# The end of two dense layers on one core: other order of the matmul passes, the last unit in two blocks, another engine for the last store

## The chip, the core and the metric

The kernel runs on one core of a Trainium2 chip. TensorE (PE) does the matrix products, and loads its weights beside them (PEld); VectorE (DVE), ScalarE (ACT) and GpSimd (POOL) do the elementwise work, SyncE (SP) issues most DMAs. Each engine takes its own instructions in the order in which they are written. The metric is the device time of one execution in microseconds (us); the kernel before takes 1350.9 us, the median of 3 runs (1350.5 to 1351.06).

## What is computed

A long convolution by Fourier transforms gives 12480 rows of 128 columns. Two dense layers follow, each of 128 to 2048 to 128:

```python
def _moe_ref(x, w_in, w_out):
    h = np.maximum(x @ w_in, 0.0)
    return (h * h @ w_out).astype(np.float32)

def _moe2_ref(x, w_in, w_out):
    h = x @ w_in
    alpha = 1.0
    g = np.where(h > 0.0, h, alpha * (np.exp(np.minimum(h, 0.0)) - 1.0))
    return (g @ w_out).astype(np.float32)
```

## The kernel before

The change lies in `phase3`, which does both dense layers. The 12480 rows are cut into NT = 25 tiles of 512 columns of the transposed data; the last tile has 334. The 2048 hidden values of a tile are done in 8 units of 256, two blocks of 128 partitions in one PSUM tile `[128, 2, n]`. So each layer has NS = 200 units.

An operand in float32 is split into a part in fp32r, hi, and the rest, lo. One product of a unit is six matmuls (`mm6`, L190 to L195): for each of the two blocks high weights by hi and low weights by hi, which makes four, and then high weights by lo for each block, which makes the last two, passes 4 and 5 (counted from 0). The first product of a unit writes `h` (`mm1`), the second adds to `y` over 8 units (`mm2`); `y` is the output of the tile. For the last tile of layer 2 the second product is not split: two matmuls in plain float32 with the whole weights `wl` (L783).

The elementwise work of one unit of layer 2, with its lines: ACT makes `tn` = tanh(h/2) (L827) and `ex` = exp(h) (L828); DVE makes `em` = (ex + 1) * tn in the place of tn (L887), which is exp(h) - 1, and `g` = max(min(em, 0), h) in the place of ex (L913); ACT copies g to fp32r, `hi` (L170); `lo` = g - hi is made by DVE, or one block by POOL and one by DVE at the end (L167). Layer 1 has r, g, hi and lo of its own (L895, L899, L906, L167).

One loop runs over s. Iteration s does unit s of layer 1 and unit k = s - 11 of layer 2, so that from s = 200 on (`both` is false) only layer 2 is left, in the units 189 to 199. In one iteration the units of layer 2 stand at four stages: the first product of k (`mid(k)`), em and g of k - 1 (`pa`), hi and lo of k - 2 (`pb`), and the second product of k - 3 (`pc`). The last tile of layer 2 is the units 192 to 199.

The order in which the code is written is the order on each engine (the schedule is manual). Two things in it matter here. `mid(k)` stands at the end of an iteration, or, where `end` is true (k from 194 on), right behind the second product of k - 3 and ahead of the elementwise work. And `lo_of` takes an argument `after`: an artificial wait of the subtraction until `em` of this iteration is done.

The PSUM tiles for h in layer 2 come from a pool of two (`h2`) and, for every third unit of the last 8 (`third`), from a third tile (`h`) that layer 1 no longer needs. The last column tile is copied out of PSUM by ACT (`fin`, L170) and stored by a DMA that SP issues (L803).

Of the kernel before, what the change touches and what calls it, by code (L numbers as in the profile page):

```python
# [14 lines left out]
AF = mybir.ActivationFunctionType  # L15
ALU = mybir.AluOpType
# [19 lines left out]
NT = len(SIZES) - 1  # L36
# [13 lines left out]
LO0 = 8  # L50
# [106 lines left out]
class Build:  # L157
# [29 lines left out]
    def big(self, i, dt=F32):  # L187
        return self.wp.tile([128, (4096, 4096, 8192)[i]], dt, tag=f"m{i}", name=f"m{i}")

    def mm6(self, outs, w, hi, lo, first, last):  # L190
        one = outs[0] is outs[1]
        seq = [(b, h, x) for b in range(2) for h, x in ((0, hi), (1, hi))] + [(b, 0, lo) for b in range(2)]
        for i, (b, h, x) in enumerate(seq):
            self.nc.tensor.matmul(outs[b], lhsT=w[:, b, h], rhs=x[b], start=first and i in ((0,) if one else (0, 2)),  # L194
                                  stop=last and i in ((5,) if one else (4, 5)))  # L195

# [467 lines left out]
    def phase3(self):  # L664
        nc, a = self.nc, self.a
        ctx0 = self.ctx
        with ExitStack() as self.ctx:
            gh = self.pool("gh3", 3)
            gp = self.pool("gp3", 2)
# [76 lines left out]
                    xin[t, 0] = (xh, xl)  # L746
                yield

            def mm1(t, l, u, odd=False):
                n, ne = width(t)  # L750
                xh, xl = xin[t, l]
                w = self.w[l, 0]
                if odd:
                    hs = spare()
                elif l == 0:
                    hs = psh.tile([128, 2, 512], F32, tag="h", name="h")
                else:
                    hs = pair.pop("s")
                self.mm6([hs[:, b, :ne] for b in range(2)], w[:, 2 * u:2 * u + 2], [xh[:, :ne]] * 2, [xl[:, :ne]] * 2,
                         True, True)  # L760
                return hs[:, :, :ne]

            def pairs(pool, nm, t, dt=F32):
                return pool.tile([128, 2, 512], dt, tag=nm, name=nm)[:, :, :width(t)[1]]
# [6 lines left out]
                        self.tc.add_manual_dep(i.ins, after.ins.name, SYNC, reason="lo beside the reads of h")  # L771
                st["lo"] = lo

            def mm2(t, l, u, hi, lo):
                n, ne = width(t)
                w = self.w[l, 1]
                if u == 0:
                    nm = f"y{l if t < NT - 1 else 0}"
                    yps[t, l] = psy.tile([128, 512], F32, tag=nm, name=nm)
                y = yps[t, l][:, :ne]  # L780
                if lo is None:
                    for b in range(2):
                        nc.tensor.matmul(y, lhsT=wl[:, 2 * u + b], rhs=hi[:, b, :ne], start=(u + b == 0),  # L783
                                         stop=(u + b == 8))
                    return
                self.mm6([y, y], w[:, 2 * u:2 * u + 2], [hi[:, b, :ne] for b in range(2)],
                         [lo[:, b, :ne] for b in range(2)], u == 0, u == 7)

            def fin(t, l):
                n, ne = width(t)  # L790
                y = yps[t, l]
                if l == 0:
                    xh, xl = row(xp, "xh1", F32R), row(xp, "xl1", F32R)
                    self.copy(xh[:, :ne], y[:, :ne])
                    yield
                    self.sub(nc.vector, xl[:, :ne], y[:, :ne], xh[:, :ne].bitcast(F32))
                    xin[t, 1] = (xh, xl)
                    return
                if t < NT - 3:
                    yield  # L800
                ys = row(ld, "ys")
                self.copy(ys[:, :n], y[:, :n])
                nc.sync.dma_start(out=self.outs(t), in_=ys[:, :n])  # L803

            seq = [(t, u) for t in range(NT) for u in range(8)]
            NS = len(seq)
# [14 lines left out]
            def mid(k, own):  # L821
                if not 0 <= k < NS:
                    return
                pair["s"] = own
                t2, u2 = seq[k]
                e = two[k] = {"t": t2, "h": mm1(t2, 1, u2), "tn": pairs(gp, "tn", t2), "ex": pairs(gh, "ex", t2)}
                nc.scalar.activation(out=e["tn"], in_=e["h"], func=AF.Tanh, scale=0.5)  # L827
                nc.scalar.activation(out=e["ex"], in_=e["h"], func=AF.Exp)  # L828

            def whole(q):  # L830
                w = self.w[1, 1][:, 2 * q:2 * q + 2].bitcast(F32)
# [6 lines left out]
            one, two = {}, {}  # L838
# [4 lines left out]
            for s in range(NS + LEAD + 2):  # L843
                k = s - LEAD
                m = s - LAG1
                both = s < NS
                pa, pb, pc = (two.get(k - i) for i in (1, 2, 3))
                pair.pop("s", None)
                pair["late"] = not both
                end = NS - 6 <= k < NS  # L850
                own = None
                if 0 <= k < NS:
                    third = k >= NS - 8 and k % 3 == (NS - 7) % 3
                    own = psh.tile([128, 2, 512], F32, tag="h", name="h") if third else spare()
                if both:
                    t, u = seq[s]
                    if own is not None:
                        pair["s"] = own
                    if (t, u) in loads:
                        load(loads[t, u])  # L860
                    if (t, u) in preps:
                        bg.append(prep(preps[t, u]))
                step()
                if both:
                    f = one[s] = {"t": t, "h": mm1(t, 0, u, k < 0 and (s == 1 or s > 0 and s % 2 == 0))}
                while post:
                    post.pop(0)()
                if 0 <= m < NS:
                    e = one.pop(m)
                    mm2(e["t"], 0, seq[m][1], e["hi"], e["lo"])  # L870
                if pc:
                    two.pop(k - 3)
                    mm2(pc["t"], 1, seq[k - 3][1], pc["hi"], pc["lo"])
                    if seq[k - 3][1] == 7:
                        late.append((pc["t"], 1))
                if end:
                    mid(k, own)
                if pb and pb["t"] == NT - 1:
                    two.pop(k - 2)
                    mm2(pb["t"], 1, seq[k - 2][1], pb["g"], None)  # L880
                    if seq[k - 2][1] == 7:
                        late.append((pb["t"], 1))
                    pb = None
                after = None
                if pa:
                    pa["em"] = pa["tn"]
                    after = nc.vector.scalar_tensor_tensor(out=pa["em"], in0=pa["ex"], scalar=1.0, in1=pa["tn"],  # L887
                                                           op0=ALU.add, op1=ALU.mult)
                if s - 1 in one:
                    lo_of(one[s - 1], "lo0", nc.gpsimd if s > LO0 else nc.vector, after=after)  # L890
                if both and t == 3:
                    whole(u)
                if both:
                    f["r"] = pairs(gp, "r", t)
                    nc.scalar.activation(out=f["r"], in_=f["h"], func=AF.Relu)  # L895
                step()
                if both:
                    f["g"] = pairs(gp, "g", t)
                    nc.vector.scalar_tensor_tensor(out=f["g"], in0=f["h"], scalar=0.0, in1=f["r"],  # L899
                                                   op0=ALU.max, op1=ALU.mult)  # L900
                if pb:
                    pb["hi"] = pairs(gh, "hi1", pb["t"], F32R)
                    self.copy(pb["hi"], pb["g"])
                if both:
                    f["hi"] = pairs(gh, "hi0", t, F32R)
                    nc.scalar.activation(out=f["hi"], in_=f["r"], func=AF.Square)  # L906
                if 0 <= m < NS and m % 8 == 7:
                    finish(seq[m][0], 0)
                if not both and pb:
                    lo_of(pb, "lo1", nc.gpsimd, (0,), after)  # L910
                if pa:
                    pa["g"] = pa["ex"]
                    nc.vector.scalar_tensor_tensor(out=pa["g"], in0=pa["em"], scalar=0.0, in1=pa["h"],  # L913
                                                   op0=ALU.min, op1=ALU.max)
                while low:
                    next(low.pop(0), 0)
                if pb:
                    lo_of(pb, "lo1", nc.vector, (slice(0, 2) if both else 1,))
                for x in late:
                    finish(*x)  # L920
                late = []
                if not end:
                    mid(k, own)
# [44 lines left out]
```

## Time and profile before

| | |
|---|---|
| median of 3 runs | 1350.9 us |
| the profiled execution | 1351.62 us |
| its span in the trace | 1349.8 us |
| PE busy | 1337.2 us, 99% of the span |
| DVE busy | 1173.7 us, 87% |
| ACT busy | 1118.8 us, 83% |
| POOL busy | 621.6 us, 46% |

The profiled execution lasted 1351.62 us; its trace spans 1349.8 us, so 1.8 us lie outside the trace. Times in rows are us from the start of the span. A matmul's end is modelled; of the matmuls therefore their starts are read. A number in brackets at the end of a row is the time for which the engine stood idle before the instruction, and whose end released it.

### The profile page before, as it was taken

The page shows a single profiled execution, that of the slowest core. Times are in us where ns is not written, and L with a number is a line of the kernel's source. Part 1 is how long each engine was busy: PE and PEld are TensorE (multiplying, and loading weights), DVE is VectorE, ACT ScalarE, POOL GpSimd, SP SyncE. Part 2 cuts the span into 40 slices and gives each one's busy share as a digit, 9 for nine tenths or more (in the row PEclk, how much of TensorE's full clock was granted, in tenths as well). Part 3 has the DMA queues.
Part 4 walks back from the last instruction along what each step waited for, and adds up shares of the span by engine and source line. Part 5 has one row for each costly group of instructions (what it writes and reads, how often), then busy time and mean ns, then how long its engine had stood idle before and what let it go on. Part 6 is the DMA issues. An engine that isn't in the chain of part 4 may idle for free.

```text
span 1349.8 us, 18810 instructions
## 1 busy us (share of the span) xinstructions
PE 1337.2 (99%) x6958; PEld 1113.9 (83%) x6958; DVE 1173.7 (87%) x1190; ACT 1118.8 (83%) x1435; POOL 621.6 (46%) x364
## 2 busy tenths in 40 slices
PE   9999999999999999999999999999999999999998
PEld 9987777898888888888888888888888888888885
DVE  6659996889989898998899889988998989898997
ACT  6678775788888898889888888988898888888885
POOL 3027780455744444444444444444444445444531
PEclk9999999999999999999999999999999999999999
DMA  8747775401110111011011101110111011100000
GB/s 253 222 138 218 217 232 155 130 3 51 52 46 7 52 52 37 17 53 53 22 31 52 53 9 44 53 52 1 53 53 49 4 53 53 35 2 9 8 8 14
DMA packets 71338, 89.36 MB, mean 66 GB/s; under 512 B 5579, under 2 KB 62790, under 8 KB 71246
## 3 DMA queue, kind: packets, MB, share of 16 engines
q1 hardware_dynamic: 71102, 88.03, 21.9%
q8 instruction: 55, 0.90, 0.3%
q14 instruction: 37, 0.30, 0.1%
q10 hardware_dynamic: 144, 0.13, 0.0%
HBM read 69.78 MB, written 18.32 MB: 65 GB/s over the span
## 4 chain that ended last, share of the span: by engine, by line
PE 91%; DMA 5%; DVE 2%; SPq 1%; issue 0%; ACT 0%; POOL 0%; DVEq 0%; ACTq 0%; POOLq 0%
PE h L194 38%; PE y L194 38%; PE v L527 3%; PE u L504 3%; PE s L318 3%; DMA m<-in_xv_dram 2%; PE h L376 2%; PE h L645 2%; PE h L649 2%; PE rt L363 1%; DMA z<-Zd 1%; DMA xr<-in_post_dram 1%; PE y L783 1%; DVE tn L887 0%; DVE lo L167 0%
## 5 line engine op out<-in xcount | busy, mean ns | idle before, releaser
L167 POOL TENSOR_TENSOR lo<-g,hi 128x1024 fp32r<-128x1024 f32 (+2 forms) x192 | 467.8, 2437 | 599.9 <-DVE tn L887 495.9
L194 PE MATMUL h<-xh,m 128*128 128x512 f32 (+3 forms) x1600 | 421.3, 385 | 3.4 <-DVE g L899 2.3
L194 PE MATMUL y<-hi,m 128*128 128x512 f32 (+2 forms) x1568 | 419.0, 389 | 0.0
L194 PEld LDWEIGHTS h<-xh,m 128*128 128x128 f32 x1600 | 298.6, 188 | 62.4 <-DVE g L899 3.3
L194 PEld LDWEIGHTS y<-hi,m 128*128 128x128 f32 x1568 | 290.0, 188 | 59.2 <-ACT ys L170 4.7
L827 ACT ACTIVATE tn<-h 128x1024 f32<-128x1024 f32 (+3 forms) x200 | 201.5, 1008 | 151.5 <-PE h L194 151.5
L887 DVE SCALAR_TENSOR_TENSOR tn<-ex,tn 128x1024 f32<-128x1024 f32 (+3 forms) x200 | 240.3, 1201 | 99.7 <-ACT ex L828 98.3
L167 DVE TENSOR_TENSOR lo<-ex,hi 128x1024 fp32r<-128x1024 f32 (+3 forms) x192 | 248.1, 1292 | 0.0
L899 DVE SCALAR_TENSOR_TENSOR g<-h,r 128x1024 f32<-128x1024 f32 (+3 forms) x200 | 238.2, 1191 | 9.3 <-ACT r L895 9.3
L194 PE MATMUL y<-lo,m 128*128 128x512 f32 (+2 forms) x784 | 240.4, 387 | 2.1 <-POOL lo L167 1.6
L194 PE MATMUL h<-xl,m 128*128 128x512 f32 (+3 forms) x800 | 242.1, 384 | 0.0
L913 DVE SCALAR_TENSOR_TENSOR ex<-tn,h 128x1024 f32<-128x1024 f32 (+3 forms) x200 | 236.7, 1184 | 1.8 <-DVE tn L887 0.5
L906 ACT ACTIVATE hi<-r 128x1024 fp32r<-128x1024 f32 (+3 forms) x200 | 209.8, 1049 | 0.5
L895 ACT ACTIVATE r<-h 128x1024 f32<-128x1024 f32 (+3 forms) x200 | 202.4, 1012 | 8.3 <-PE h L194 6.9
L170 ACT ACTIVATE hi<-ex 128x1024 fp32r<-128x1024 f32 (+2 forms) x192 | 203.8, 1062 | 0.0
L828 ACT ACTIVATE ex<-h 128x1024 f32<-128x1024 f32 (+3 forms) x200 | 199.6, 998 | 0.0
L194 PEld LDWEIGHTS y<-lo,m 128*128 128x128 f32 x784 | 146.6, 188 | 34.6 <-POOL lo L167 3.7
L194 PEld LDWEIGHTS h<-xl,m 128*128 128x128 f32 x800 | 149.5, 188 | 28.5
L519 POOL TENSOR_TENSOR pt<-pt 127x256 f32<-127x256 f32 x43 | 33.5, 779 | 88.4 <-DVE pt L516 88.3
L516 DVE TENSOR_TENSOR pt<-u,hh 127x512 f32<-127x512 f32 (+1 forms) x46 | 31.2, 679 | 21.4 <-PE u L504 20.5
L527 PE MATMUL v<-pt,g 127*128 127x512 f32 (+1 forms) x92 | 48.5, 612 | 0.0
L724 DVE SCALAR_TENSOR_TENSOR v<-z,sg 118x384 f32<-118x384 f32 (+3 forms) x75 | 43.0, 573 | 0.0
(87 smaller groups left out, 1058.9 us busy)
## 6 DMA issues: line engine op xcount, KB each, us to landing
Zd<-z SPq DMA_DIRECT2D x45, 256.0 KB
z<-Zd SPq DMA_DIRECT2D x48, 192.0 KB
z<-Zd SPq DMA_DIRECT2D x48, 136.5 KB
xc<-in_xv_dram SPq DMA_DIRECT2D x16, 392.0 KB
tb<-in_tf_dram SPq DMA_DIRECT2D x46, 127.0 KB
out_dram<-ys SPq DMA_DIRECT2D x22, 256.0 KB
raw<-in_moe_w_in_dram SPq DMA_DIRECT2D x8, 512.0 KB
raw<-in_moe_w_out_dram SPq DMA_DIRECT2D x8, 512.0 KB
```

The costliest lines, as they stand in the source:

```text
L167: return eng.tensor_tensor(out=out, in0=a, in1=b, op=ALU.subtract)
L170: self.nc.scalar.activation(out=out, in_=in_, func=AF.Copy)
L194: self.nc.tensor.matmul(outs[b], lhsT=w[:, b, h], rhs=x[b], start=first and i in ((0,) if one else (0, 2)), stop=last and i in ((5,) if on ...
L527: nc.tensor.matmul(v, lhsT=self.g[:N2], rhs=pt.rearrange("p j r d -> p (j r d)"), start=True, stop=True)
L724: nc.vector.scalar_tensor_tensor(out=v[:k, i, q], in0=zi[:, :, 1], scalar=self.sg[:k, i:i + 1], in1=zi[:, :, 0], op0=ALU.mult, op1=ALU.add)
L827: nc.scalar.activation(out=e["tn"], in_=e["h"], func=AF.Tanh, scale=0.5)
L828: nc.scalar.activation(out=e["ex"], in_=e["h"], func=AF.Exp)
L887: after = nc.vector.scalar_tensor_tensor(out=pa["em"], in0=pa["ex"], scalar=1.0, in1=pa["tn"], op0=ALU.add, op1=ALU.mult)
L895: nc.scalar.activation(out=f["r"], in_=f["h"], func=AF.Relu)
L899: nc.vector.scalar_tensor_tensor(out=f["g"], in0=f["h"], scalar=0.0, in1=f["r"], op0=ALU.max, op1=ALU.mult)
L906: nc.scalar.activation(out=f["hi"], in_=f["r"], func=AF.Square)
L913: nc.vector.scalar_tensor_tensor(out=pa["g"], in0=pa["em"], scalar=0.0, in1=pa["h"], op0=ALU.min, op1=ALU.max)
```

## The change

The order of instructions differs from the iteration s = 200 on; ahead of it nothing moves.

- Once layer 1 is done (`both` false), the second product of k - 3 is cut in two: its four hi passes, then `mid(k)`, then its two lo passes.
- `end` is true from k = 190 on, not from 194, so that `mid(k)` stands ahead of the elementwise work in four more iterations. The third PSUM tile is used from k = 190 on.
- `after` is left out for lo of layer 1's last unit.
- The last unit (199) is done block by block: its first product in the order of passes 0, 1, 4, 2, 3, 5, then tn and ex of block 0 and of block 1, then em and g of block 0 and of block 1.
- The last store is issued by ACT, not by SP.

```diff
-    def mm6(self, outs, w, hi, lo, first, last):
+    def mm6(self, outs, w, hi, lo, first, last, passes=range(6)):
         one = outs[0] is outs[1]
         seq = [(b, h, x) for b in range(2) for h, x in ((0, hi), (1, hi))] + [(b, 0, lo) for b in range(2)]
-        for i, (b, h, x) in enumerate(seq):
+        for i in passes:
+            b, h, x = seq[i]
...
-                nc.sync.dma_start(out=self.outs(t), in_=ys[:, :n])
+                (nc.sync if t < NT - 1 else nc.scalar).dma_start(out=self.outs(t), in_=ys[:, :n])
...
-                e = two[k] = {"t": t2, "h": mm1(t2, 1, u2), "tn": pairs(gp, "tn", t2), "ex": pairs(gh, "ex", t2)}
-                nc.scalar.activation(out=e["tn"], in_=e["h"], func=AF.Tanh, scale=0.5)
-                nc.scalar.activation(out=e["ex"], in_=e["h"], func=AF.Exp)
+                order = (0, 1, 4, 2, 3, 5) if k == NS - 1 else range(6)
+                e = two[k] = {"t": t2, "h": mm1(t2, 1, u2, passes=order), "tn": pairs(gp, "tn", t2),
+                              "ex": pairs(gh, "ex", t2)}
+                for b in blocks(k):
+                    nc.scalar.activation(out=e["tn"][:, b], in_=e["h"][:, b], func=AF.Tanh, scale=0.5)
+                    nc.scalar.activation(out=e["ex"][:, b], in_=e["h"][:, b], func=AF.Exp)
+
+            def blocks(k):
+                return (0, 1) if k == NS - 1 else (slice(0, 2),)
+
+            def minmax(e, b):
+                nc.vector.scalar_tensor_tensor(out=e["g"][:, b], in0=e["em"][:, b], scalar=0.0, in1=e["h"][:, b],
+                                               op0=ALU.min, op1=ALU.max)
...
-                end = NS - 6 <= k < NS
+                end = NS - 10 <= k < NS
                 own = None
                 if 0 <= k < NS:
-                    third = k >= NS - 8 and k % 3 == (NS - 7) % 3
+                    third = k >= NS - 10 and k % 3 == (NS - 7) % 3
...
                 if pc:
                     two.pop(k - 3)
-                    mm2(pc["t"], 1, seq[k - 3][1], pc["hi"], pc["lo"])
+                    mm2(pc["t"], 1, seq[k - 3][1], pc["hi"], pc["lo"], range(6) if both else range(4))
+                if end:
+                    mid(k, own)
+                if pc:
+                    if not both:
+                        mm2(pc["t"], 1, seq[k - 3][1], pc["hi"], pc["lo"], (4, 5))
                     if seq[k - 3][1] == 7:
                         late.append((pc["t"], 1))
-                if end:
-                    mid(k, own)
...
-                    after = nc.vector.scalar_tensor_tensor(out=pa["em"], in0=pa["ex"], scalar=1.0, in1=pa["tn"],
-                                                           op0=ALU.add, op1=ALU.mult)
+                    pa["g"] = pa["ex"]
+                    for b in blocks(k - 1):
+                        after = nc.vector.scalar_tensor_tensor(out=pa["em"][:, b], in0=pa["ex"][:, b], scalar=1.0,
+                                                               in1=pa["tn"][:, b], op0=ALU.add, op1=ALU.mult)
+                        if k == NS:
+                            minmax(pa, b)
                 if s - 1 in one:
-                    lo_of(one[s - 1], "lo0", nc.gpsimd if s > LO0 else nc.vector, after=after)
+                    lo_of(one[s - 1], "lo0", nc.gpsimd if s > LO0 else nc.vector, after=after if both else None)
```

On TensorE, in the iterations k = 190 and 191, there stood before (y1 is the output of tile 23, hi1 and lo1 are the parts of one unit, and h2_12016 and h2_12050 the first products of units 190 and 191):

```order
L194 MATMUL y1_11909<-hi1_12000,m2_2011 128x512 x4
L194 MATMUL y1_11909<-lo1_12002,m2_2011 128x512 x2
L194 MATMUL h2_12016<-xh1_11698,m2_2011 128x512 x4
L194 MATMUL h2_12016<-xl1_11699,m2_2011 128x512 x2
L194 MATMUL y1_11909<-hi1_12030,m2_2011 128x512 x4
L194 MATMUL y1_11909<-lo1_12035,m2_2011 128x512 x2
L194 MATMUL h2_12050<-xh1_11698,m2_2011 128x512 x4
```

and there stands now (h_12016 and h2_12050 are the same two products; hi1_12040 is what hi1_12030 was):

```order
L195 MATMUL y1_11909<-hi1_12000,m2_2011 128x512 x4
L195 MATMUL h_12016<-xh1_11698,m2_2011 128x512 x4
L195 MATMUL h_12016<-xl1_11699,m2_2011 128x512 x2
L195 MATMUL y1_11909<-lo1_12002,m2_2011 128x512 x2
L195 MATMUL y1_11909<-hi1_12040,m2_2011 128x512 x4
L195 MATMUL h2_12050<-xh1_11698,m2_2011 128x512 x4
L195 MATMUL h2_12050<-xl1_11699,m2_2011 128x512 x2
```

The lo passes have moved from ahead of h to behind it. Between the six matmuls of h_12016 and the hi passes that need hi1_12040 two matmuls are left; the hi passes stand directly ahead of the next h.

On ScalarE, in the same iterations, there stood before:

```order
L827 ACTIVATE tn_12012<-h2_11984 128x1024
L828 ACTIVATE ex_12013<-h2_11984 128x1024
L170 ACTIVATE hi1_12030<-ex_11981 128x1024
L170 ACTIVATE xh1_12032<-y0_11723 128x334
L827 ACTIVATE tn_12046<-h2_12016 128x1024
L828 ACTIVATE ex_12047<-h2_12016 128x1024
L170 ACTIVATE hi1_12058<-ex_12013 128x1024
```

and there stands now:

```order
L831 ACTIVATE tn_12012<-h2_11984 128x1024
L832 ACTIVATE ex_12013<-h2_11984 128x1024
L831 ACTIVATE tn_12033<-h_12016 128x1024
L832 ACTIVATE ex_12034<-h_12016 128x1024
L170 ACTIVATE hi1_12040<-ex_11981 128x1024
L170 ACTIVATE xh1_12042<-y0_11723 128x334
L831 ACTIVATE tn_12061<-h2_12050 128x1024
```

The copy hi1 of unit 188 (from ex_11981, which holds its g) stood ahead of tn and ex of unit 190; now it stands behind them. The same holds in the three iterations that follow (hi1_12068, hi1_12092, hi1_12116).

On VectorE, at the very end, two rows over both blocks stood before:

```order
L887 SCALAR_TENSOR_TENSOR tn_12199<-ex_12200,tn_12199 128x2x334
L913 SCALAR_TENSOR_TENSOR ex_12200<-tn_12199,h2_12192 128x2x334
L887 SCALAR_TENSOR_TENSOR tn_12214<-ex_12215,tn_12214 128x2x334
L913 SCALAR_TENSOR_TENSOR ex_12215<-tn_12214,h_12207 128x2x334
L962 UNCONDITIONAL_BRANCH
```

and now four stand there:

```order
L838 SCALAR_TENSOR_TENSOR ex_12200<-tn_12199,h2_12192 128x2x334
L903 SCALAR_TENSOR_TENSOR tn_12214<-ex_12215,tn_12214 128x334
L838 SCALAR_TENSOR_TENSOR ex_12215<-tn_12214,h_12207 128x334
L903 SCALAR_TENSOR_TENSOR tn_12214<-ex_12215,tn_12214 128x334
L838 SCALAR_TENSOR_TENSOR ex_12215<-tn_12214,h_12207 128x334
```

The last unit's em and g are made for block 0 and then for block 1.

## Rows read from the trace of the kernel before

**Rows 1.** Part 1 of the page: busy us, share of the span, instructions.

```profile
PE 1337.2 (99%) x6958; PEld 1113.9 (83%) x6958; DVE 1173.7 (87%) x1190; ACT 1118.8 (83%) x1435; POOL 621.6 (46%) x364
```

**Rows 2.** Busy time by stretch: us; PE, PEld, DVE, ACT, POOL; PEclk granted clock; DMA, GB/s.

```profile
1320.00:1324.00 4.00, 3.26 (x13) 2.10 (x12) 3.11 (x4) 3.70 (x5) 1.29 (x1) 1.00 0.00 0
...
1347.00:1349.80 2.80, 0.00 (x0) 0.00 (x0) 0.00 (x0) 0.07 (x1) 0.00 (x0) 1.00 0.17 61
```

**Rows 3.** Timeline, PE and ACT, units 190 and 191: start, us, instruction, idle before.

```profile
1317.42 1.09 PE L194 MATMUL h<-xh,m 128*128 128x512 f32 x4
...
1318.81 1.08 PE L194 MATMUL y<-hi,m 128*128 128x512 f32 x4
1319.01 1.03 ACT L827 ACTIVATE tn<-h 128x1024 f32<-128x1024 f32 x1 [1.79 <-PE h L194]
...
1319.94 1.01 ACT L828 ACTIVATE ex<-h 128x1024 f32<-128x1024 f32 x1
...
1320.62 1.09 PE L194 MATMUL h<-xh,m 128*128 128x512 f32 x4
1320.83 1.06 ACT L170 ACTIVATE hi<-ex 128x1024 fp32r<-128x1024 f32 x1
...
1322.00 1.15 PE L194 MATMUL y<-hi,m 128*128 128x512 f32 x4
```

**Rows 4.** Timeline, PE and ACT, units 192 to 194, 334 columns.

```profile
1325.73 0.73 ACT L827 ACTIVATE tn<-h 128x668 f32<-128x668 f32 x1 [0.64 <-PE h L194]
1326.36 0.72 ACT L828 ACTIVATE ex<-h 128x668 f32<-128x668 f32 x1
...
1326.96 1.06 ACT L170 ACTIVATE hi<-ex 128x1024 fp32r<-128x1024 f32 x1
...
1327.80 0.77 PE L194 MATMUL h<-xh,m 128*128 128x334 f32 x4
...
1328.71 1.08 PE L194 MATMUL y<-hi,m 128*128 128x512 f32 x4
...
1330.58 0.77 PE L194 MATMUL h<-xh,m 128*128 128x334 f32 x4
```

**Rows 5.** Timeline, POOL, DVE and PE, end of layer 1.

```profile
1308.89 1.64 POOL L167 TENSOR_TENSOR lo<-g,hi 128x668 fp32r<-128x668 f32 x1 [2.94 <-DVE tn L887]
...
1310.56 1.22 DVE L167 TENSOR_TENSOR lo<-ex,hi 128x1024 fp32r<-128x1024 f32 x1
...
1311.96 0.63 PE L194 MATMUL y<-lo,m 128*128 128x512 f32 x2
...
1312.10 1.23 DVE L887 SCALAR_TENSOR_TENSOR tn<-ex,tn 128x1024 f32<-128x1024 f32 x1 [0.33 <-ACT ex L828]
...
1313.79 0.77 PE L194 MATMUL y<-hi,m 128*128 128x334 f32 x4
...
1315.06 1.75 POOL L167 TENSOR_TENSOR lo<-ex,hi 128x512 fp32r<-128x512 f32 x1
...
1315.16 0.57 PE L194 MATMUL y<-lo,m 128*128 128x334 f32 x2 [0.60 <-POOL lo L167]
...
1315.97 1.92 DVE L887 SCALAR_TENSOR_TENSOR tn<-ex,tn 128x1024 f32<-128x1024 f32 x1 [0.32 <-ACT ex L828]
```

**Rows 6.** Timeline: the only DMA that ACT issues, and the last instructions.

```profile
0.73 0.40 ACTq L266 DMA_DIRECT2D xt<-in_wz_dram  x1
...
1342.24 0.85 DVE L913 SCALAR_TENSOR_TENSOR ex<-tn,h 128x668 f32<-128x668 f32 x1
...
1343.33 0.85 DVE L887 SCALAR_TENSOR_TENSOR tn<-ex,tn 128x668 f32<-128x668 f32 x1 [0.24 <-ACT ex L828]
1344.29 0.85 DVE L913 SCALAR_TENSOR_TENSOR ex<-tn,h 128x668 f32<-128x668 f32 x1
...
1345.20 1.39 PE L783 MATMUL y<-ex,wl 128*128 128x334 f32 x4 [0.66 <-DVE ex L913]
...
1347.10 0.33 SPq L803 DMA_DIRECT2D out_dram<-ys  x1
```

More of the change, by code (lines that the diff above doesn't have):

```diff
@@ L747, in prep, with mm1 @@
                 yield
-            def mm1(t, l, u, odd=False):
+            def mm1(t, l, u, odd=False, passes=range(6)):
                 n, ne = width(t)
@@ L759, in mm1 @@
                 self.mm6([hs[:, b, :ne] for b in range(2)], w[:, 2 * u:2 * u + 2], [xh[:, :ne]] * 2, [xl[:, :ne]] * 2,
-                         True, True)
+                         True, True, passes)
                 return hs[:, :, :ne]
@@ L772, in lo_of, with mm2 @@
                 st["lo"] = lo
-            def mm2(t, l, u, hi, lo):
+            def mm2(t, l, u, hi, lo, passes=range(6)):
                 n, ne = width(t)
                 w = self.w[l, 1]
-                if u == 0:
+                if u == 0 and 0 in passes:
                     nm = f"y{l if t < NT - 1 else 0}"
@@ L786, in mm2 @@
                 self.mm6([y, y], w[:, 2 * u:2 * u + 2], [hi[:, b, :ne] for b in range(2)],
-                         [lo[:, b, :ne] for b in range(2)], u == 0, u == 7)
+                         [lo[:, b, :ne] for b in range(2)], u == 0, u == 7, passes)
             def fin(t, l):
@@ L910, in phase3 @@
                     lo_of(pb, "lo1", nc.gpsimd, (0,), after)
[L911 to L914, printed above, removed]
+                if pa and k < NS:
+                    minmax(pa, slice(0, 2))
                 while low:
```

## The prediction

> **What bounds the kernel now.** I read the page's busy shares first: PE is busy 99% of the span, and the next engine, DVE, 87% [rows 1]. For most of the span the time is PE's own work, and there the change moves nothing. So I went to the last 40 us, by stretches. In the four us from 1320 PE is busy for 3.26, with 13 matmuls, beside 3.70 of ACT [rows 2]: here PE waits for the elementwise engines, and an order matters. Then I read the timeline of this stretch, to see for each wait what ended last.
>
> Two places carry the argument. At the end of layer 1 PE reaches the lo passes of layer 1 and waits for POOL: the hi passes start at 1313.79, the lo passes only at 1315.16, released by POOL's lo [rows 5]. And in the units behind, each iteration of layer 2 is a loop through three engines, whose lengths stand in the timeline: the first product starts at 1317.42, its tn on ACT at 1319.01, ex at 1319.94, a hi copy at 1320.83, and the hi passes that read this copy start at 1322.00 [rows 3]. That is 4.58 us from the h of unit 190 to the hi passes that read the copy behind its tn and ex. Today PE fills this with the hi and lo passes of another unit and with the h of unit 191, which starts at 1320.62 [rows 3]. The reader is to see that PE loses little here because a whole h stands between the two.
>
> **The change part by part.**
>
> *The four iterations k = 190 to 193.* Because `mid` is ahead of the elementwise work there, ACT now does tn and ex of unit k first and the hi copy of unit k - 2 behind them. PE, in the next iteration, needs that very copy for its first four matmuls, and the h of unit k + 1 stands behind these. So a ring closes: h(k), tn(k), ex(k), hi(k-2), the hi passes, h(k+1). Nothing in it can overlap; only two lo passes stand between h(k) and the wait. Its length with 512 columns, from rows: the six matmuls of h 1.39 (1317.42 to 1318.81), to tn 0.20, tn to ex 0.93, ex to hi 0.89, the copy 1.06, to the hi passes 0.11 [rows 3]. Together 4.58, as read above. The four hi passes add 0.92, six matmuls of 512 taking 1.39, and I add 0.05, an estimate, for the restart of a PE that had waited: 5.55 us. With 334 columns h takes 0.91 (1327.80 to 1328.71), tn to ex 0.63, ex to hi 0.60, the rest as above [rows 4]: 0.91 + 0.20 + 0.63 + 0.60 + 1.06 + 0.11 + 0.97 = 4.48. From the h of unit 190 to that of 194 there are two rings of each kind: 11.10 + 8.96 = 20.06 us. Before, the same way took from 1317.42 to 1330.58, 13.16 us [rows 3, 4]. **This term is +6.90 us.** The lo passes that were moved behind h are now hidden, as meant, but what they hide behind is a longer wait. DVE and POOL have time to spare in a ring: em and g of 512 columns and half a lo are about 1.2 + 1.2 + 0.7 us.
>
> *The lo passes of unit 191, two matmuls.* They now stand between h of unit 194 and the first float32 passes, where PE is the bound: two of six matmuls, +0.46 us.
>
> *POOL's lo of layer 1's last unit without the wait.* Its operands are ready, so it can start when POOL's lo before it ends, at 1308.89 + 1.64 = 1310.53 [rows 5]. PE then no longer waits at 1315.16: from 1313.79 four matmuls of 334 (0.61), two (0.31), four of 512 (0.92), and h of unit 190 could start at 1315.64 in place of 1317.42, because the lo passes are no longer ahead of it: -1.78 us. But at 1310.56 DVE starts its own lo with two operands in SBUF [rows 5], and the trace shows what such a pair does: em at 1315.97 took 1.92 beside POOL's lo, which ran from 1315.06 to 1316.81, while the one at 1312.10 took 1.23 [rows 5]. One waits for the other. If POOL is first, DVE's lo ends at about 1313.25 (1310.53 + 1.64 + 1.22, less the 0.14 that the pair at 1315.97 overlapped) and PE's lo passes slip from 1311.96 to 1313.31, and all behind by this and a restart: h of unit 190 at 1317.08, only -0.34. If DVE is first, em slips instead and h keeps the 1315.64. The starts lie 0.03 apart, which no row decides. I take the middle, **-1.06**, and keep both ends.
>
> *The last unit by blocks.* Before, em starts at 1343.33, g at 1344.29, PE at 1345.20 with 1.39 us for both blocks [rows 6]. Now half of h is ready three matmuls earlier, so that DVE is the limit: it is free at 1342.24 + 0.85 = 1343.09 [rows 6]. Four instructions on 334 columns: 1.22 us for 1024 and 0.85 for 668 make about 0.50 for 334, an estimate. With 0.1 between em and the g that reads it, and a next one that starts 0.1 before the end of the last, DVE ends at about 1345.15, as before. But PE then has only one block left, 0.70 in place of 1.39. **-0.65**; the ends are 0 (if DVE's four take longer by as much) and -0.9.
>
> *The last store from ACT.* SP issues it at 1347.10 in 0.33 us; ACT's only DMA took 0.40 to issue [rows 6]. What is lost is this 0.07, what is saved one hand-over from ACT to SP, which the trace shows as no wait of its own. I take 0; the ends are +0.1 and -0.1, the size of the hand-over from ACT's copy to PE in the ring.
>
> *Sum.* 6.90 + 0.46 - 1.06 - 0.65 = **+5.65 us**, with the two starts of POOL 4.9 and 6.4. The profiled execution lasted 1351.62, its trace 1349.8, so the same execution would last 1357.2. It lies 0.7 above the median of the runs, 1350.9; on that scale 1356.5.
>
> *TensorE's clock.* In the rings PE is busy for about half of the time, with pauses of up to 2.8 us (5.55 less 2.31 of h and hi passes and 0.46 of lo passes). The granted clock was 1.00, the upper level of 2.4 GHz, both in the stretch at 1320 with its waits and in the 2.8 us at the end in which PE did nothing [rows 2]; so the sum leaves the clock alone. The Trainium skill, "TensorE: Matmul & The Clock Gate", section "A second HAM failure mode: psum-queue depth-cycling", says that short idle times between groups of matmuls can make the clock switch between its two levels. By that rule the time would be that of rival A; no row of before shows such a switch.
>
> **The rivals.**
>
> *A: the clock falls in the rings.* Place: units 191 to 194. If the granted clock goes to 1.2 GHz after the first ring, matmuls take twice as long: +2.31 for the second ring, +1.83 for each of the two of 334 columns (0.91 + 0.92), and about two units behind, until it is back, each with 0.91 for h and 1.39 for the two float32 passes [rows 4, 6], +4.6. Together +10.6, so 1367. For it speaks that pauses come four times in a row; against it that the clock stayed at 1.00 through 2.8 us of idle PE [rows 2].
>
> *B: the copy is not late, faster.* Place: ACT's hi copies. If ACT reached each copy by the time PE has done h(k) and the lo passes, the rings would not bind, and what is left is the earlier start of unit 190 and the blocks: -1.78 - 0.65 = -2.4, so 1348.5. It decides at this point: behind h(k) PE has 0.46 us of work, while ACT needs 0.20 + 0.93 + 0.89 + 1.06 = 3.08 from the end of h(k) to the end of the copy [rows 3]. It would have to do the copy, whose g is ready an iteration earlier, ahead of tn(k); that the engine takes in program order speaks against it: at 1319.01 ACT had stood idle for 1.79 us waiting for h.
>
> *C: half of it.* If PE or ACT finds work in the rings that I don't see, and each costs less than a third of the 1.7 us that I give it, gains and losses meet: 6.90 would shrink to about 2, and the sum to 1 or below, within 0.2% of before (2.7 us). Nothing in the rows speaks for it.
>
> **How the numbers follow.** The forecast, a loss of 4.9 to 6.4 us plus the small bounds, has 0.82 and alone would lie in 1355 to 1358. A has 0.08, B 0.06, C 0.04. About 0.2% (2.7 us) is what a measurement of this kernel can tell from no change. So faster 0.06, same 0.04, slower 0.90. The range that leaves out A, B and C but gives the forecast room for a ring that I measured wrongly by 0.5 us each is 1353.5 to 1360.
>
> **What would show it.** Right: in the trace after, h starts of units 190 to 194 lie 5.5, 5.5, 4.5 and 4.5 us apart, PE is idle for 2 to 2.8 us ahead of four groups of hi passes, released by ACT's hi copy, and ACT's tn waits for h each time; DVE is no longer busy without a gap. POOL's lo of 668 starts near 1310.5, and it or DVE's lo beside it is longer by about 1.5 us. At the end the last float32 passes come as two pairs, and the store follows the copy on ACT. Wrong: if PE's waits for ACT's copy are below 1 us (B), if the granted clock in these stretches is below 1.00 (A), or if the four distances together are below 16 us.

## The result and the profile after

The changed kernel takes 1360.6 us, the median of 6 runs (1358.55 to 1365.45); the kernel before, beside it, 1350.95 (1350.47 to 1351.98). The ratio is 1.0075 with a 95% interval of 1.0064 to 1.0085: slower by 9.65 us by the medians. The forecast was 1356.5 with a range to 1360.0. The direction was right and the size was not; the measured time lies above the range.

The profiled execution lasted 1359.13 us with a span of 1357.3. Executions differ by up to some four us in the stretch ahead of the change, so I compare what follows one landmark that the change doesn't touch: the store of tile 22, which SP issues at 1301.06 before and at 1299.88 after (in the profiled executions of all runs, between 1299.61 and 1303.89). These are its two rows, before and after:

```profile
1301.06 0.33 SPq L803 DMA_DIRECT2D out_dram<-ys  x1
...
1299.88 0.33 SPq L804 DMA_DIRECT2D out_dram<-ys  x1
```

From this landmark to the end of the span it is 48.74 us before and 57.42 after, +8.68. This is one execution of each; the one after lies 1.5 us below the median of its six runs.

The ring that the prediction described is there. The rows of the timeline that answer to [rows 3], PE and ACT, units 190 and 191, of the kernel after:

```profile
1315.89 1.08 PE L195 MATMUL h<-xh,m 128*128 128x512 f32 x4
...
1317.26 0.61 PE L195 MATMUL y<-lo,m 128*128 128x512 f32 x2
1317.46 1.02 ACT L831 ACTIVATE tn<-h 128x1024 f32<-128x1024 f32 x1 [1.27 <-PE h L195]
...
1318.38 1.02 ACT L832 ACTIVATE ex<-h 128x1024 f32<-128x1024 f32 x1
1319.28 1.06 ACT L170 ACTIVATE hi<-ex 128x1024 fp32r<-128x1024 f32 x1
...
1320.39 1.19 PE L195 MATMUL y<-hi,m 128*128 128x512 f32 x4 [2.52 <-ACT hi L170]
...
1321.42 1.08 PE L195 MATMUL h<-xh,m 128*128 128x512 f32 x4
```

From h to the hi passes it is 4.50 us (4.58 in [rows 3]), and from h to h 5.53. PE stands idle for 2.52 us ahead of the hi passes. The view of the waits, from 1309 to the end (who waited for whom, us in total, times, longest), counts four of them:

```profile
PE y L195 <- ACT hi L170: 8.4, 4, 2.5
```

In the timeline these four are 2.52, 2.52, 1.87 and 1.52 us, where the prediction had 2 to 2.8. The other distances are longer than the sum had them: h of units 191 to 194 starts at 1321.42, 1327.67, 1333.01 and 1338.29, so 6.25, 5.34 and 5.28 us apart where 5.55, 4.48 and 4.48 were expected. The rows of units 192 to 194, and the first float32 passes behind them:

```profile
1327.67 1.31 PE L195 MATMUL h<-xh,m 128*128 128x334 f32 x4
...
1333.01 1.32 PE L195 MATMUL h<-xh,m 128*128 128x334 f32 x4
...
1338.29 0.78 PE L195 MATMUL h<-xh,m 128*128 128x334 f32 x4
...
1339.69 1.29 PE L784 MATMUL y<-ex,wl 128*128 128x334 f32 x4
```

The busy times by stretch (us; PE, PEld, DVE, ACT, POOL; granted clock; DMA, GB/s) show why:

```profile
1320.00:1322.00 2.00, 1.61 (x7) 1.35 (x8) 1.29 (x2) 0.68 (x2) 1.30 (x1) 1.00 0.00 0
...
1324.00:1326.00 2.00, 0.07 (x1) 0.07 (x1) 0.85 (x2) 1.87 (x3) 0.05 (x1) 1.00 0.00 0
1326.00:1328.00 2.00, 2.00 (x6) 1.62 (x7) 2.00 (x2) 0.00 (x0) 1.74 (x1) 0.52 0.00 0
1328.00:1330.00 2.00, 2.00 (x8) 1.62 (x7) 1.87 (x2) 0.41 (x1) 0.00 (x0) 0.62 0.00 0
1330.00:1332.00 2.00, 0.13 (x2) 0.08 (x1) 0.27 (x2) 1.87 (x3) 0.00 (x0) 1.00 0.00 0
1332.00:1334.00 2.00, 2.00 (x8) 1.77 (x9) 2.00 (x2) 0.00 (x0) 1.73 (x1) 0.73 0.00 0
1334.00:1336.00 2.00, 1.74 (x6) 1.01 (x4) 1.30 (x2) 1.08 (x2) 0.00 (x0) 0.50 0.00 0
1336.00:1338.00 2.00, 0.74 (x3) 0.66 (x4) 0.76 (x2) 1.21 (x2) 0.66 (x1) 0.92 0.00 0
```

The granted clock, 1.00 throughout this stretch before, falls to the lower level, 0.50 of 2.4 GHz, twice: from 1326, behind the second pause, and from 1333, behind the third. Behind the first pause, as long as the second, it is still 1.00. It comes back between, and from 1338 on it is 1.00 to the end. So the event of rival A came beside the ring of the forecast.

POOL's lo of layer 1's last unit and DVE's lo collide, POOL first (timeline; [rows 5] is the same place before). POOL's two instructions of 668 run without a gap, DVE's lo takes 2.66 us where it took 1.22, and PE waits 1.18 us for it:

```profile
1307.72 3.24 POOL L167 TENSOR_TENSOR lo<-g,hi 128x668 fp32r<-128x668 f32 x2 [2.93 <-DVE tn L903]
...
1309.38 2.66 DVE L167 TENSOR_TENSOR lo<-ex,hi 128x1024 fp32r<-128x1024 f32 x1
...
1312.09 0.73 PE L195 MATMUL y<-lo,m 128*128 128x512 f32 x2 [1.18 <-DVE lo L167]
```

And the end, which answers to [rows 6]:

```profile
1350.34 0.85 DVE L838 SCALAR_TENSOR_TENSOR ex<-tn,h 128x668 f32<-128x668 f32 x1
...
1351.75 0.50 DVE L838 SCALAR_TENSOR_TENSOR ex<-tn,h 128x334 f32<-128x334 f32 x1
...
1352.70 0.50 DVE L838 SCALAR_TENSOR_TENSOR ex<-tn,h 128x334 f32<-128x334 f32 x1
...
1354.13 0.45 ACT L170 ACTIVATE ys<-y 128x334 f32<-128x334 f32 x1 [2.62 <-PE y L784]
...
1354.61 0.35 ACTq L804 DMA_DIRECT2D out_dram<-ys  x1
```

From the start of g of unit 198 (the first row) to the start of ACT's last copy it is 3.79 us; before it was 4.38, from 1342.24 in [rows 6] to the copy, whose row before was:

```profile
1346.62 0.45 ACT L170 ACTIVATE ys<-y 128x334 f32<-128x334 f32 x1 [3.32 <-PE y L783]
```

From that copy to the end of the span it is 3.17 us after and 3.18 before: in these two executions the engine that issues the store makes no difference.

### The profile page after: what moved, and what is told of

Read it like the earlier page. It is cut to its first block, busy times and chain, and to the rows that moved or that the text cites. A ratio compares the mean times of both kernels' runs of the same rounds, so it can differ in the third digit from the quotient of the medians.

```text
span 1357.3 us, 18819 instructions
## 1 busy us (share of the span) xinstructions
PE 1338.9 (99%) x6958; PEld 1117.8 (82%) x6958; DVE 1178.0 (87%) x1192; ACT 1118.4 (82%) x1437; POOL 622.6 (46%) x364
## 4 chain that ended last, share of the span: by engine, by line
PE 94%; DVE 2%; ACT 1%; DMA 1%; SPq 1%; issue 1%; POOL 0%; DVEq 0%; ACTq 0%
PE h L195 38%; PE y L195 38%; PE s L319 4%; PE v L528 3%; PE u L505 3%; PE h L646 2%; PE h L377 2%; PE h L650 2%; PE rt L364 1%; PE s L285 1%; DVE lo L167 1%; DVE g L917 1%; DVE tn L903 0%; PE y L784 0%; DVE ex L838 0%
## 5 line engine op out<-in xcount | busy, mean ns | idle before, releaser
L831 ACT ACTIVATE tn<-h 128x1024 f32<-128x1024 f32 (+4 forms) x201 | 201.7, 1003 | 161.2 <-PE h L195 161.2
L903 DVE SCALAR_TENSOR_TENSOR tn<-ex,tn 128x1024 f32<-128x1024 f32 (+4 forms) x201 | 243.0, 1209 | 97.9 <-ACT ex L832 96.7
L838 DVE SCALAR_TENSOR_TENSOR ex<-tn,h 128x1024 f32<-128x1024 f32 (+4 forms) x201 | 237.4, 1181 | 1.8 <-PE h L195 0.5
L832 ACT ACTIVATE ex<-h 128x1024 f32<-128x1024 f32 (+4 forms) x201 | 199.8, 994 | 0.0
```

Source lines behind the costliest of these rows:

```text
L831: nc.scalar.activation(out=e["tn"][:, b], in_=e["h"][:, b], func=AF.Tanh, scale=0.5)
L832: nc.scalar.activation(out=e["ex"][:, b], in_=e["h"][:, b], func=AF.Exp)
L838: nc.vector.scalar_tensor_tensor(out=e["g"][:, b], in0=e["em"][:, b], scalar=0.0, in1=e["h"][:, b], op0=ALU.min, op1=ALU.max)
L903: after = nc.vector.scalar_tensor_tensor(out=pa["em"][:, b], in0=pa["ex"][:, b], scalar=1.0, in1=pa["tn"][:, b], op0=ALU.add, op1=ALU.mult)
```

## The experiments

Seven kernels ran. "Behind the landmark" is the time from the store of tile 22 to the end of the span, and "h 190 to h 194" the time between the starts of the first products of these two units, both in the one profiled execution of each kernel. The ratio is to the kernel before as it ran beside each: median 1350.95 for the kernel after, 1351.13 for 1 to 4, 1351.04 for 5 to 7.

| kernel | median us | ratio, 95% interval | behind the landmark | h 190 to h 194 |
|---|---|---|---|---|
| before | 1350.95 | | 48.74 | 13.16 |
| after | 1360.6 | 1.0075, 1.0064 to 1.0085 | 57.42 | 22.40 |
| 1 hi copy first | 1350.64 | 0.9993, 0.9984 to 1.0001 | 48.22 | 12.81 |
| 2 pauses filled | 1357.64 | 1.0045, 1.0033 to 1.0057 | 55.09 | 20.09 |
| 3 order of 190 to 193 as before | 1350.57 | 0.9994, 0.9985 to 1.0002 | 48.31 | 12.85 |
| 4 hi copy first, POOL's wait kept | 1350.07 | 0.9989, 0.9980 to 0.9997 | 47.56 | 12.78 |
| 5 as 4, lo passes ahead of h | 1353.55 | 1.0020, 1.0011 to 1.0028 | 51.29 | 16.41 |
| 6 before, with the blocks alone | 1350.42 | 0.9996, 0.9987 to 1.0005 | 48.17 | 13.16 |
| 7 two pauses filled | 1358.37 | 1.0060, 1.0047 to 1.0072 | 56.42 | 21.39 |

**1. The hi copy ahead of tn and ex.** The changed kernel, with the copy of unit k - 2 moved in ACT's order only:

```diff
                 if end:
+                    if pb and pb["t"] < NT - 1:
+                        pb["hi"] = pairs(gh, "hi1", pb["t"], F32R)
+                        self.copy(pb["hi"], pb["g"])
                     mid(k, own)
...
-                if pb:
+                if pb and "hi" not in pb:
                     pb["hi"] = pairs(gh, "hi1", pb["t"], F32R)
```

> The changed kernel with one edit: in the iterations k = 190 to 193 ACT's hi copy of unit k - 2 stands ahead of tn and ex of unit k; everything else stays (lo passes behind h, third PSUM tile, POOL's lo without the wait, blocks, last store from ACT). Theory R (the ring h(k), tn(k), ex(k), hi(k-2), hi passes, h(k+1) makes the loss, and the pauses that it leaves let the clock fall): the distances from h of unit 190 to that of 194 fall from 22.4 us in all to about 12.7 (2.8, 3.6, 3.3, 3.0), PE waits for ACT's copy less than 0.5 us in all, the granted clock is 1.00 throughout, and the time is about 1350.3, that is 0.6 below the kernel before (of it -0.6 from the blocks). Rival L (the lo passes behind h, or the PSUM tiles in another turn, make the loss): the time stays at 1356 or above.

Measured 1350.64 (0.3 above the time expected), 10 us below the changed kernel, by moving four instructions of ACT. PE's timeline from h of unit 190 on:

```profile
1316.67 1.08 PE L195 MATMUL h<-xh,m 128*128 128x512 f32 x4
...
1318.05 0.61 PE L195 MATMUL y<-lo,m 128*128 128x512 f32 x2
1318.51 1.07 PE L195 MATMUL y<-hi,m 128*128 128x512 f32 x4
1319.41 1.07 PE L195 MATMUL h<-xh,m 128*128 128x512 f32 x4
...
1321.73 0.50 PE L195 MATMUL y<-lo,m 128*128 128x512 f32 x1 [0.56 <-DVE lo L167]
```

The hi passes follow the lo passes at once, and PE no longer waits for ACT's copy. The h distances are 2.74, 3.58, 3.36 and 3.13 us, and the clock is 1.00 in every stretch up to the last matmul. Rival L falls: neither the lo passes behind h nor the third PSUM tile make the loss.

**2. The pauses filled with matmuls.** The changed kernel with its ring, and work for PE in the pause; the added products are overwritten by the next h. `nxt`, new in this run, is the next unit's PSUM tile, taken one iteration earlier.

```diff
+                    if NS - 10 <= k < NS - 6:
+                        third = (k + 1) % 3 == (NS - 7) % 3
+                        nxt = psh.tile([128, 2, 512], F32, tag="h", name="h") if third else spare()
+                        tk, uk = seq[k]
+                        ne = width(tk)[1]
+                        for i in range(10 if ne == 512 else 12):
+                            nc.tensor.matmul(nxt[:, i % 2, :ne], lhsT=self.w[1, 0][:, 2 * uk + i % 2, 0],
+                                             rhs=xin[tk, 1][0][:, :ne], start=True, stop=True)
```

> The changed kernel, with matmuls that do nothing useful put into PE's pauses: behind the lo passes of the iterations k = 190 to 193 ten of 512 columns (2.3 us) or twelve of 334 (1.84 us), into the PSUM tile that the next h overwrites. The ring stays. Theory K (what lies between the forecast and the measured 1360.6 is the granted clock that falls in the pauses): the clock stays at 1.00, the h starts lie 5.5, 5.5, 4.5 and 4.5 us apart, and the time is 1356.5 to 1357.5, with the runs within 1 us of each other. Rival S (the clock is no part of it; something else in the rings is longer): 1360 as without the filling, or more, since the matmuls add to PE's work.

Measured 1357.64, just above the expected 1356.5 to 1357.5, the runs within 1.1 us of each other. 44 more matmuls make the kernel 3.0 us faster. The ring in the timeline (L898 are the added matmuls):

```profile
1317.29 1.08 PE L195 MATMUL h<-xh,m 128*128 128x512 f32 x4
...
1319.13 2.43 PE L898 MATMUL h<-xh,m 128*128 128x512 f32 x10
...
1321.81 1.20 PE L195 MATMUL y<-hi,m 128*128 128x512 f32 x4 [0.25 <-ACT hi L170]
1322.85 1.07 PE L195 MATMUL h<-xh,m 128*128 128x512 f32 x4
...
1328.38 0.78 PE L195 MATMUL h<-xh,m 128*128 128x334 f32 x4
...
1332.88 0.78 PE L195 MATMUL h<-xh,m 128*128 128x334 f32 x4
...
1337.38 0.78 PE L195 MATMUL h<-xh,m 128*128 128x334 f32 x4
```

and its stretches where the changed kernel's clock fell:

```profile
1326.00:1332.00 6.00, 5.65 (x30) 4.57 (x29) 4.48 (x5) 3.59 (x5) 1.87 (x2) 1.00 0.00 0
1332.00:1338.00 6.00, 5.90 (x32) 5.17 (x33) 4.91 (x5) 2.29 (x3) 3.24 (x2) 1.00 0.01 3
```

The ring alone is 5.56, 5.53, 4.50 and 4.50 us, together 20.09. So most of what lies between forecast and result is the clock, which stays at 1.00 here; rival S falls. In the profiled executions the fall cost 57.42 - 55.09 = 2.33 us, all but 0.02 of it between h of unit 190 and that of 194 (22.40 - 20.09 = 2.31); by the medians it is 3.0.

**3. The order of units 190 to 193 as before.** The changed kernel with two conditions put back:

```diff
-                end = NS - 10 <= k < NS
+                end = NS - 6 <= k < NS
...
-                    third = k >= NS - 10 and k % 3 == (NS - 7) % 3
+                    third = k >= NS - 8 and k % 3 == (NS - 7) % 3
```

> The changed kernel with the two conditions end and third as before (k from 194 on, and from 192 on), so that the order of PE and ACT in k = 190 to 193 is that of before; POOL's lo without the wait, the blocks and the store from ACT stay. Theory R: no ring and clock 1.00; DVE's lo of 1024 or POOL's lo beside it is longer by 1.3 us and takes what POOL's earlier start gives (together 0 to +0.2); with the blocks -0.6 the time is 1350.3 to 1350.6. Rival P (the collision of POOL and DVE is a good part of the loss): 1352 or above.

Measured 1350.57, within 0.6 of the kernel before. The whole loss goes with these two lines, and POOL's early start with its collision gains nothing here: behind the landmark -0.43, of which the blocks are -0.57 (run 6). Rival P falls.

**4. The copy first, and POOL's wait kept.** As run 1, and:

```diff
-                    lo_of(one[s - 1], "lo0", nc.gpsimd if s > LO0 else nc.vector, after=after if both else None)
+                    lo_of(one[s - 1], "lo0", nc.gpsimd if s > LO0 else nc.vector, after=after)
```

> As the run with the copy ahead (hi first), and POOL's lo of layer 1's last unit waits for em again, as in the kernel before. Theory R with the collision as a term of its own: the h of unit 190 starts 0.7 us earlier than with the collision (DVE's lo of 1024 back at 1.22 us, PE waits for POOL's lo instead, 0.7), so about 1349.7, 1.2 below the kernel before. Rival: POOL's earlier start is worth more than the collision costs, and this is slower than the run with the copy ahead alone by 0.7 or more.

Measured 1350.07, ratio 0.9989 (0.9980 to 0.9997): faster than both kernels, though by a tenth of a percent only against the kernel before, and 0.4 above the time expected. Behind the landmark it is 0.66 below run 1 and 1.18 below the kernel before, where 0.7 and 1.2 were expected. In the timeline DVE's lo has its 1.22 us back and POOL's lo comes later:

```profile
1310.34 1.22 DVE L167 TENSOR_TENSOR lo<-ex,hi 128x1024 fp32r<-128x1024 f32 x1
...
1313.25 1.62 POOL L167 TENSOR_TENSOR lo<-g,hi 128x668 fp32r<-128x668 f32 x1 [2.93 <-DVE tn L906]
```

So leaving out POOL's wait is itself a loss of some 0.6 us beside the rest of the change.

**5. As 4, with the lo passes ahead of h again.**

```diff
-                    mm2(pc["t"], 1, seq[k - 3][1], pc["hi"], pc["lo"], range(6) if both else range(4))
+                    mm2(pc["t"], 1, seq[k - 3][1], pc["hi"], pc["lo"], range(6))
...
-                    if not both:
-                        mm2(pc["t"], 1, seq[k - 3][1], pc["hi"], pc["lo"], (4, 5))
```

> The kernel with the hi copy ahead and POOL's wait kept (the fourth run), with the two lo passes of k - 3 back ahead of the h of unit k. Theory R (with the copy in its right place, PE's waits for lo are what the split hides): h of unit 190 starts about 0.9 us later, the distances from unit 190 to 194 add up to about 15 us instead of 12.8, PE waits for POOL's and DVE's lo, and the time is 2 to 3 us above the fourth run, about 1352.5. Rival D (DVE is the bound of this stretch in any order, so that where the lo passes stand costs nothing): within 0.5 us of the fourth run, 1350.1 to 1350.6.

Measured 1353.55, 3.5 above run 4, where 2 to 3 were expected. One wait of PE is the centre of it, with the clock falling behind it (timeline, then stretches):

```profile
1321.04 0.50 PE L195 MATMUL y<-lo,m 128*128 128x512 f32 x1 [2.38 <-DVE lo L167]
1321.37 1.75 PE L195 MATMUL h<-xh,m 128*128 128x512 f32 x4
```

```profile
1320.00:1322.00 2.00, 0.96 (x3) 0.81 (x4) 2.00 (x3) 0.79 (x1) 0.00 (x0) 0.89 0.00 0
1322.00:1324.00 2.00, 2.00 (x6) 1.54 (x5) 1.87 (x3) 0.00 (x0) 1.28 (x1) 0.50 0.00 0
```

So the split hides the waits for lo, once ACT's copy is early. A single long wait was enough for the clock to fall here. The h distances add up to 16.41 where 15 were expected; here too I had left the clock out.

**6. The blocks alone.** The kernel before with the edits of the last unit (`passes`, `blocks`, `minmax`) and nothing else.

> The kernel before with one part of the change, the last unit by blocks (first product in the order 0, 1, 4, 2, 3, 5; tn, ex, em and g for block 0 and then for block 1). Theory: DVE ends as before, PE has only one block behind it, 0.6 us less: from the start of g of unit 198 to the last copy on ACT 3.8 us instead of 4.4; the time about 1350.4. Rival: the smaller instructions cost DVE what PE gains, and the distance stays 4.4 us.

Measured 1350.42, ratio 0.9996 (0.9987 to 1.0005): by the time not to be told from no change. The trace shows it: from g of unit 198 to the last copy 3.78 us, 0.60 less than before.

```profile
1341.71 0.85 DVE L838 SCALAR_TENSOR_TENSOR ex<-tn,h 128x668 f32<-128x668 f32 x1
...
1345.49 0.45 ACT L170 ACTIVATE ys<-y 128x334 f32<-128x334 f32 x1 [2.59 <-PE y L784]
```

**7. Only the first two pauses filled.** As run 2, but:

```diff
-                    if NS - 10 <= k < NS - 6:
+                    if NS - 10 <= k < NS - 8:
```

> The changed kernel with PE's pauses filled in the iterations k = 190 and 191 only, where they are longest (2.5 us); those behind h of units 192 and 193 (2.1 us) stay. Theory K (the clock falls because of such pauses, the shorter ones too): the granted clock is below 1.00 somewhere between h of unit 193 and the last tile, though later than without any filling, and the time lies between 1357.6 and 1360.6. Rival M (only the two longest pauses make it fall): clock 1.00 throughout, h starts 5.5, 5.5, 4.5 and 4.5 apart, 1357.2 to 1357.7 as with all four filled.

Measured 1358.37, inside the range of theory K. The clock falls, later than without filling, behind the pause of 1.90 us that ends at 1330.54, a little ahead of the place expected (h of unit 193 starts at 1332.10):

```profile
1326.00:1330.00 4.00, 2.60 (x12) 1.97 (x12) 3.84 (x3) 1.80 (x3) 1.80 (x1) 1.00 0.00 0
1330.00:1332.00 2.00, 1.46 (x4) 1.23 (x5) 1.78 (x3) 0.49 (x1) 1.38 (x1) 0.74 0.00 0
1332.00:1334.00 2.00, 2.00 (x8) 1.91 (x8) 1.87 (x2) 0.00 (x0) 0.35 (x1) 0.50 0.00 0
```

Rival M falls. In this profiled execution the two pauses cost 1.33 us (56.42 - 55.09).

## Why the prediction was right in its direction and wrong in its size

- *The ring.* Right to the tenth: 20.06 us forecast, 20.09 with the clock at 1.00 (run 2). Its cause is shown by run 1: the place of four copies in ACT's order, and nothing else, closes it.
- *The lo passes of unit 191.* Forecast +0.46. From h of unit 194 to the first float32 passes it is 1.40 after (1338.29 to 1339.69); the h of 334 columns alone takes 0.91 [rows 4]. +0.49.
- *POOL's lo.* The collision was described as it happened, with POOL first. The middle that I took, -1.06, was between the two ends; the trace gave the end of -0.34: h of unit 190 lies 16.36 us behind the landmark before and 16.01 after, -0.35. This term was mis-sized by 0.7. With POOL's wait kept, h of unit 190 lies 15.41 behind the landmark (run 4), -0.95: what is gained comes from the lo passes moved behind h, and leaving out the wait takes 0.6 of it back.
- *The blocks.* -0.65 forecast, -0.59 in the trace, -0.57 in run 6.
- *The store.* 0 forecast, 0.01 measured.
- *The clock.* This step failed: "so the sum leaves the clock alone". The clock fell, and with it the 1357.64 of run 2 became 1360.6: a term of 2.3 us between the two traces, 3.0 by the medians, that the sum had at nothing. I had given this to rival A with a chance of 0.08, on the ground that the clock was 1.00 through the 2.8 us of idle PE at the end of the span [rows 2]. That was the wrong row to rest on: one pause with nothing behind it says little of a stretch in which work and pauses take turns, and no row of before showed such a stretch. Rival A had the event and the place but a price of 10.6: it let the clock stay down for three rings and two more units, while in the trace it came back in the middle and was 1.00 again by 1338, at a cost of 2.3 us in that execution. The rule that was cited from the Trainium skill, "TensorE: Matmul & The Clock Gate", section "A second HAM failure mode: psum-queue depth-cycling", agrees with the trace after: the clock went between its two levels, 0.50 and 1.00, twice in 12 us, here at pauses that come from the wait for ACT's copy.

The terms without the clock, with the measured collision, make 6.90 + 0.46 - 0.34 - 0.65 = 6.37; run 2 shows 55.09 - 48.74 = 6.35. By the medians 4.0 us lie between the forecast +5.65 and the measured +9.65: 0.7 is the collision, some 3 the clock. The six runs of the changed kernel spread over 6.9 us and the five of run 2 over 1.1; the kernel before spread over 1.5 in its six runs beside the changed kernel, but over 5.0 in its 29 runs beside runs 1 to 4, so the spread is not shown to be the clock's at the end alone.

Not settled: why the clock costs more in some runs (1365.45) than in others. The runs without a profile show only the mean clock of the whole execution (0.992 in that run, 0.996 in the profiled one), and this mean holds falls elsewhere too. In the profiled execution of the changed kernel the clock also fell near 217 us, far ahead of the change, at a pause of 1.12 us; in that of the kernel before the same pause left it at 1.00. The stretch before and after:

```profile
210.00:220.00 10.00, 8.72 (x51) 7.72 (x51) 2.95 (x11) 2.21 (x5) 0.00 (x0) 1.00 0.39 132
...
210.00:220.00 10.00, 8.72 (x47) 8.20 (x47) 2.63 (x9) 2.22 (x5) 0.00 (x0) 0.84 0.43 138
```

Of the 21 runs of the kernel before beside runs 5 to 7, 11 have a mean of 0.998. So whether the clock falls at a given pause differs from one execution to the next, and one trace in which it stayed at 1.00 does not show that it always does; that it does so in runs 1 and 2 rests on the times of their eleven and five executions as well. The 2.33 us are read behind the landmark and hold nothing of this stretch; the 3.0 of the medians may.

## What to carry to other kernels

When a product is moved ahead on one engine, write down the ring that it closes through the others, with each engine's program order: an instruction that was early on its own engine (here ACT's hi copy) becomes late by being written behind work that depends on the moved product. If a change makes TensorE pause between groups of matmuls, once (run 5) or again and again, price the lower clock as a term of the sum, not as a far rival; filling the pauses with matmuls whose results are overwritten tells the clock from the wait. Four copies in another place took away the whole loss of 0.75% (run 1); with POOL's wait kept as well it became the version with the lowest median here (run 4).

## What the runs showed of the hardware

The granted clock fell to 0.50 behind pauses of 1.87 to 2.52 us between groups of matmuls (runs 5 and 7, and the kernel after), though PE was at work between the pauses. Not every such pause did it: behind the first of 2.52 us in the kernel after it stayed at 1.00, and so it did for 2.8 us after the last work of PE in the kernel before. Near 217 us, a pause of 1.12 us came with a fall to 0.50 in the kernel after and with none in the kernel before. A subtraction on POOL and one on DVE, each with two operands in SBUF, came nearly one behind the other: 1.22 us on DVE became 2.66 beside a POOL instruction of 1.62, which had started first (runs 1 and 3 as well, 2.66 and 2.65).
